# Reordering the weight conversions that run beside the first MLP block, and moving one of them out of the forward transform

## The chip, the core and the metric

The kernel runs on one core of one Trainium2 chip. The metric is the device time of one execution in microseconds (us). Five engines with queues of their own matter here: TensorE (PE, matrix products), VectorE (DVE), ScalarE (ACT), GpSimd (POOL) and SyncE (SP, which only issues transfers).

## The reference, cut to what matters

```python
X = np.fft.rfft(x, axis=1)                      # x: 2 x 3008 x 256
Yr = Xr @ w_r - Xi @ w_i + b_r                  # channel mixing in frequency
Yi = Xr @ w_i + Xi @ w_r + b_i
Yr, Yi = soft_threshold(Yr, 0.01), soft_threshold(Yi, 0.01)
y = np.fft.irfft(Yr + 1j * Yi, n=3008, axis=1)  # 6016 tokens of 256
h = y @ w_in1; y = (h * sigmoid(1.702 * h)) @ w_out1   # 256 -> 2048 -> 256
h = y @ w_in2; y = (h * sigmoid(h)) @ w_out2
```

The four MLP weights are float64 in memory.

## The kernel before

Every product is done in three passes over a rounded part and a remainder (hi x hi, hi x lo, lo x hi). The program has four stages: the forward transform (16 groups g), the mixing (12 units i), the inverse transform (16 steps), and the two MLP layers. PE's order is the order in which the code is written in the MLP; in the transforms a scheduler places the instructions of most engines, except where the code pins an engine's order (POOL and SP in the forward transform, SP in the mixing, PE in the inverse transform). From the second group of the MLP on, all engines follow the written order.

**The MLP.** The tokens are cut into blocks i of 1,024 (the last has 896), and each layer's 2,048 hidden columns into 8 pairs p of 256. A group (layer, block, pair) forms its four hidden quarters from 7 instead of 8 block products: seven products of 3 matmuls (L772), and, for the group before, the second product in 8 pieces of 3 matmuls (L744), so 45 matmuls. Around them: L791 on ACT copies the first product out of PSUM, L793 on DVE adds the second to it (the first hidden quarter). L801 and L803 on ACT copy two more products, and L809 and L812 on DVE add to them. Each quarter then goes through the activation (L775, ACT), is rounded (L777, ACT), and L782 subtracts to get the remainder: on POOL for three quarters, on DVE for one. PE can't go on with the product that reuses a PSUM bank before L803 has emptied it.

**The conversions.** The weights come as 64-bit words, and 32 units (one pair of `w_in` or `w_out` of a layer) are turned into float32 beside the other work, in this order: `w_in` pairs 0 to 3, `w_out` 0 to 4, `w_in` 4 to 7, `w_out` 5 to 7 of layer 1, then layer 2. One unit is a load `raw` from memory (L144 with L145, or L148; SP issues it, there is **one** buffer), L157 on ACT, five bit operations L162 to L166 on DVE, of which L164 and L166 read `raw`, and the final add L219 on POOL. The next unit's load can't start before L166 is done with `raw`. A unit of layer 1 that is kept in SBUF is placed one group later: for `w_in` four small DVE operations L194 to L197 make sums, and L98 (ACT) with L99 (POOL) split it into hi and lo; `w_out` needs L98 and L99 alone. The other units are written back to memory and fetched later.

`CFG['tf']`, `['tm']` and `['ti']` say behind which forward groups, mixing units and inverse steps one unit is converted; `kb` and `kr` do the same for the pairs of the first MLP block and of the later ones (pairs 1 to 6; pairs 1, 3, 5 and 6). The helper `pump(k)` issues k of the five bit operations that wait in the list `fill`, `settle` issues L219, and `hook(h)` is called at six places in a group, with `hook(4)` issuing the next load.

Of the kernel before, what the change touches and what calls it, by code (L numbers as in the profile page):

```python
# [8 lines left out]

F32 = mybir.dt.float32  # L10
CFG = {'lv0': 'V', 'lv': 'VVVVVPVVVVVP', 'dd0': 'VPVVPPPPPVVP', 'dd': 'VVVVVVVVVVPV', 'mpl': 'VPPVVP', 'ths': 'VVVVPV', 'thf': 'PVPVVPVV', 'fsl': 'VPVVVVPV', 'ivf': 'PVVPVVVVVPPVPPVV', 'cva': 'P', 'pol': 'PPPP', 'pil': 'P', 'mvl': 'PVVP', 'xl': 'V', 'xse': 'V', 'gl': 'VPPPPPPP', 'tf': [6, 9, 12], 'tm': [2, 4, 7], 'ti': [2, 5, 9, 13], 'kb': [0, 1, 1, 1, 1, 1, 1, 0], 'kr': [0, 1, 0, 1, 0, 1, 1, 0], 'fa': 3, 'fe': 2, 'xp': [2, 4, 4, 5], 'xq': [1, 4, 1], 'xs': 4, 'xi': [11, 12, 13, 15], 'xsi': 9, 'ca': 4, 'tl': True, 'fwd': 'Pool,SP', 'rest0': 'all', 'rest1': 'all', 'last1': 'all', 'inv': 'PE', 'mid': 'SP', 'last0': 'all', 'thm': 'A', 'gl0': 'PVPVVVPV', 'gl2': 'PPPPPPPP', 'gl3': 'PPPPPPPV', 'xl0': 'V', 'xl1': 'V', 'pre': 17, 'pre2': 0, 'yd': 6, 'nf': 4, 'lvb': 6, 'mlp': 'none', 'pr': 'VVVP', 'pf': 'PV', 'eo': '0000', 'ddb': 6, 'mlp1': 'all', 'mlp2': 'all'}
NUM = dict(tf=[5, 9, 13], tm=[1, 3, 5, 7, 9, 11], ti=[0, 2, 4, 6, 8, 10, 12, 14, 14, 15, 15], kb=[2] * 8, kr=1, fa=3, fe=2, pm=0, nf=4, lvb=6, ddb=8, ivb=1, eob=2, fsb=6, f1=3, f2=0, fm=[7, 8, 9], fi=[1, 1, 2, 2], pre=13, pre2=1, yd=3, psh=0, ie=[12], xp=[1, 3, 4, 5], xq=[1, 2, 2], xs=5, nw=4, xi=[14, 14, 15, 15], xsi=13, rw=2, ca=4, cc=2, tb=1, tmn=1)

DEF = dict(pr="V", pf="V", lv0="V", lv="VPP", dd0="VVVVVP", dd="VPV", mpl="PV", ths="VP", thf="VVPP", fsl="VP", ivf="PPVV", cva="P", pol="P", pil="P", mvl="V", xl="PPVVPPP", xl0="PPVVPPP", xl1="PPVVPPP", xse="VP", gl="P", gl0="P", gl2="P", gl3="P", wcl="V", thc="V", thm="V")
# [7 lines left out]
P = 128  # L22
# [34 lines left out]
def spectral_mlp_kernel(ctx, tc, xin, m0, mfwd, minv, wc, bias, w_in1, w_out1, w_in2, w_out2, outT):  # L57
    nc = tc.nc
# [73 lines left out]
    loaded, bits, added, fill = [], [], [], []  # L132
# [69 lines left out]

    wib_p = []
# [12 lines left out]
    def settle():  # L216
        pump()
        for u, (a, c) in bits:
            E('cva', u[2]).tensor_add(a, a, c)  # L219
            if not u[3]:  # L220
                spilled[u[:3]] = d = dram_p.tile([P, 2 * CU], F32, name=f"w_{u[0]}{u[1]}_{u[2]}")
                nc.sync.dma_start(out=d, in_=a)
        fresh = [(u, a) for u, (a, _) in bits if u[3]]
        done, added[:] = added[:], fresh
        bits[:] = []
        return done

    def window(k, done, now=False):
        for u, a in done:
            if u[0] == "in":  # L230
                for part in place_in(u[1], u[2], a, E('pil', u[2]), sums_tmp):
                    if now:
                        for f in part:
                            f()
                    else:
                        fill.extend(part)
            else:
                place_out(u[1], u[2], a, E('pol', u[2]))
        for _ in range(min(k, len(loaded))):
            u, raw = loaded.pop(0)  # L240
            bits.append((u, cv_bits(raw)))
# [20 lines left out]
    raws, lvs, xs = {}, {}, {}  # L262
# [497 lines left out]
    def group(l, i, p, hook):  # L760
        t0, n = blocks[i]
        func = AF.Silu if l else AF.Gelu_apprx_sigmoid
        w = w_in[l, p]

        y = [[yt[:, mm, t0 + h * n : t0 + (h + 1) * n] for h in range(2)] for mm in range(2)]

        def prod(ps, s, k, first=True):

            xh, xl = xb[l, i, k]
            a, z = w[:, 0, s], w[:, 1, s]  # L770
            for m, (st, mv) in enumerate(((a, xh), (a, xl), (z, xh))):
# [12 lines left out]

        (y1, y3), (y2, y4) = y
        begun = (l, i, p) != (0, 0, 0)
        X, Z, Y = (bank(0, "x")[:, :n] for _ in range(3))
        prod(X, 0, 0)  # L790
        nc.scalar.copy(y1, X)  # L791
        prod(Y, 1, 1)
        nc.vector.tensor_add(y1, y1, Y)  # L793
        hook(1)
        if begun:
            out_next()
        rest(nc.gpsimd, *gate(0, 0, y1))
        hook(2)
        pump(3)
        prod(Z, 3, 2)  # L800
        nc.scalar.copy(y2, Z)  # L801
        prod(X, 4, 3, False)
# [45 lines left out]
    puts = []  # L848
# [12 lines left out]
    for at, (l, i, p) in enumerate(seq):  # L861
        if (l, i, p) in ((0, 0, 1), (0, 0, 2)):
            region(f'mlp{p}')
        if (i, p) == (1, 0):
            region(f'rest{l}')
        if (i, p) == (last, 0):
            region(f'last{l}')
        nxt = (l, i + 1) if i < last else (1, 0)
        more = p == NPR - 1 and (l, i) != (1, last)
        k = rate(at)  # L870

        def hook(h):
            if more:
                if h in (1, 2):
                    for x in ((0,), (1, 2))[h - 1]:
                        xprep(*nxt, x)
                if h == 3:
                    xprep(*nxt, 3, 1)
                if h == 4:
                    xprep(*nxt, 3, 2)  # L880
            if p == 0 and h < 4:
                xprep(l, i, {1: 4, 2: 6, 3: 5}[h])
            if h == 1 and p == NPR - 2 and (l, i) != (1, last):
                xsums(*nxt)
            if h == (3 if len(done) < 2 else 1):
                window(0, done, True)
                done[:] = []
            if h == 1:
                window(k, ())
            if h in (2, 3):  # L890
                moved(h)
            if h == 5:
                fetched[:] = fetch_for(at + 1)
            if h == 4:
                pump()
                cv_load(1 - len(loaded))
            if h == 6:
                done.extend(settle())
                done.extend(added)
                added[:] = []  # L900

        group(l, i, p, hook)
        if (l, i, p) == (0, 0, 0):
            while ydone:
                inv_out()
            closed("iv", "fs")
            wib_p.append(opened("wib", "left", NPR // 2))
        if N('pre2') and (l, i, p) == (0, last, NPR - 1):
            tc.keep_in_program_order(nc.scalar.preload_act_table(AF.Silu))
# [150 lines left out]
```

## Time and profile before

| | us |
|---|---|
| median of three runs (1248.66 to 1253.36) | 1251.43 |
| profiled execution, device time | 1253.26 |
| span of its instructions | 1251.5 |
| PE busy in the span | 1187.8 |
| DVE, ACT, POOL busy | 698.2, 775.6, 587.8 |

The span is divided so: forward transform to about 79, mixing to 158, inverse transform to 220, MLP from 220 to the end. An idle time in brackets in a timeline row is what the engine waited just before that instruction, and for whom.

### The profile page before, as it was taken

How to read it: one execution, taken by the hardware profiler on the slowest of the kernel's cores; microseconds unless marked ns; L12 is line 12 of the kernel's file. 1: busy time of each engine (PE TensorE's matmuls, PEld its weight loads, DVE VectorE, ACT ScalarE, POOL GpSimd, SP SyncE). 2: the span in 40 equal slices, each digit the busy share in tenths (PEclk: the TensorE clock that was granted, in tenths of full speed). 3: DMA queues.
4: the chain of work that ended last, by engine and by line, in shares of the span. 5: the costliest groups of instructions: out<-in, count | busy, mean ns of one | idle time of the engine just before them, and what ended most of it. 6: DMA issues, size and time to landing. Idle time of an engine off the chain costs nothing.

```text
span 1251.5 us, 14934 instructions
## 1 busy us (share of the span) xinstructions
PE 1187.8 (95%) x5220; PEld 969.8 (77%) x5220; DVE 698.2 (56%) x1034; ACT 775.6 (62%) x1481; POOL 587.8 (47%) x465
## 2 busy tenths in 40 slices
PE   7879888777999999999999999999999999999998
PEld 4868678556787887887878987878888888888897
DVE  7899999866735646447446463352352442623522
ACT  3555433656766766767667777666675665765764
POOL 4585553555544444445455774433333333333342
PEclk9989989988999999999999999999999999999999
DMA  8452123011011001001011110000000000000000
GB/s 310 161 183 68 51 71 129 25 46 39 17 49 44 26 34 52 26 26 52 26 59 35 34 43 26 1 32 3 1 35 1 1 34 1 19 16 1 34 1 30
DMA packets 27277, 57.57 MB, mean 46 GB/s; under 512 B 2369, under 2 KB 11585, under 8 KB 25922
## 3 DMA queue, kind: packets, MB, share of 16 engines
q1 hardware_dynamic: 25154, 41.94, 10.2%
q0 software_dynamic: 2048, 14.68, 3.2%
q8 instruction: 41, 0.67, 0.2%
q14 instruction: 34, 0.28, 0.1%
HBM read 44.94 MB, written 11.67 MB: 45 GB/s over the span
## 4 chain that ended last, share of the span: by engine, by line
PE 71%; DVE 15%; ACT 6%; issue 3%; DMA 3%; POOL 1%; SPq 0%; DVEq 0%; ACTq 0%; POOLq 0%
PE o L744 37%; PE x L772 32%; ACT yt L775 1%; DVE f L533 1%; DVE fl L99 1%; PE psf L357 1%; DMA raw<-in_wi 1%; DMA raw<-in_wo 1%; DVE th L519 1%; ACT g L777 1%; DVE cv_c L166 1%; DVE cv_c L165 1%; DVE yt L664 1%; DVE g L782 1%; DVE cv_a L164 1%
## 5 line engine op out<-in xcount | busy, mean ns | idle before, releaser
L782 POOL TENSOR_TENSOR g<-yt,g 128x512 fp32r<-128x512 f32 (+1 forms) x288 | 384.5, 1347 | 538.6 <-DVE g L782 167.5
L744 PE MATMUL o<-g,wo 128*128 128x512 f32 (+1 forms) x2304 | 575.1, 392 | 1.0 <-POOL g L782 0.8
L772 PE MATMUL x<-x,wi 128*128 128x512 f32 (+1 forms) x2016 | 514.0, 394 | 26.5 <-ACT yt L803 22.1
L744 PEld LDWEIGHTS o<-g,wo 128*128 128x128 f32 x2304 | 434.0, 188 | 97.0 <-POOL g L782 1.2
L772 PEld LDWEIGHTS x<-x,wi 128*128 128x128 f32 x2016 | 378.0, 189 | 118.4 <-ACT yt L803 27.8
L775 ACT ACTIVATE yt<-yt 128x512 f32<-128x512 f32 (+1 forms) x288 | 178.9, 621 | 263.4 <-DVE yt L809 216.8
L777 ACT CAST g<-yt 128x512 fp32r<-128x512 f32 (+1 forms) x384 | 234.2, 612 | 11.8
L809 DVE TENSOR_TENSOR yt<-yt,x 128x512 f32<-128x512 f32 (+1 forms) x96 | 64.7, 674 | 264.1 <-PE x L772 264.1
L793 DVE TENSOR_TENSOR yt<-yt,x 128x512 f32<-128x512 f32 (+1 forms) x96 | 64.7, 674 | 143.2 <-ACT yt L791 142.2
L782 DVE TENSOR_TENSOR g<-yt,g 128x512 fp32r<-128x512 f32 (+1 forms) x96 | 68.8, 717 | 69.5 <-ACT g L777 68.5
L695 DVE TENSOR_TENSOR x<-yt,x 128x512 fp32r<-128x512 f32 (+1 forms) x48 | 53.5, 1114 | 24.2 <-ACT x L692 24.2
L812 DVE TENSOR_TENSOR yt<-yt,x 128x512 f32<-128x512 f32 (+1 forms) x96 | 64.8, 675 | 1.9 <-PE x L772 0.5
L775 ACT ACTIVATE yt<-x 128x512 f32<-128x512 f32 (+1 forms) x96 | 56.0, 584 | 3.7 <-PE x L772 3.7
L791 ACT COPY yt<-x 128x512 f32<-128x512 f32 (+1 forms) x96 | 54.8, 571 | 2.6 <-PE x L772 2.5
L803 ACT COPY yt<-x 128x512 f32<-128x512 f32 (+1 forms) x96 | 55.6, 579 | 0.6 <-PE x L772 0.6
L801 ACT COPY yt<-x 128x512 f32<-128x512 f32 (+1 forms) x96 | 54.7, 570 | 0.0
L219 POOL TENSOR_TENSOR cv_a<-cv_a,cv_c 128x512 f32<-128x512 f32 x32 | 47.0, 1469 | 15.9 <-DVE cv_c L166 12.4
L360 PE MATMUL psi<-m,fh 128*128 128x376 f32 (+3 forms) x208 | 49.8, 329 | 2.6 <-DVE sd L514 2.1
L157 ACT ACTIVATE cv_c<-raw 128x512 f32<-128x512 f32 x32 | 21.6, 674 | 43.8 <-DMA raw<-in_wo 23.7
L501 PE MATMUL psm<-wc_hi,xtl 128*128 128x512 f32 x96 | 38.6, 407 | 5.3 <-DVE xtl L99 5.3
L501 PE MATMUL psm<-wc_hi,xth 128*128 128x512 f32 x96 | 39.5, 412 | 3.7 <-ACT xth L98 3.7
L360 PE MATMUL psi<-m,fl 128*128 128x376 f32 (+3 forms) x104 | 34.8, 334 | 6.1 <-DVE fl L99 5.2
(108 smaller groups left out, 1065.7 us busy)
## 6 DMA issues: line engine op xcount, KB each, us to landing
raw<-in_wi SPq DMA_DIRECT2D x32, 256.0 KB, 3.1
raw<-in_wo SPq DMA_DIRECT2D x16, 512.0 KB, 3.6
raw<-in_x SPq DMA_DIRECT2D x12, 512.0 KB, 6.6
out_t<-yt SPq DMA_DIRECT2D x20, 256.0 KB, 2.0
m<-in_mf POOLq DMA_DIRECT2D x4, 1128.0 KB, 7.4
m<-in_mi POOLq DMA_DIRECT2D x4, 1128.0 KB, 7.6
w_out<-cv_a SPq DMA_DIRECT2D x13, 256.0 KB, 2.0
cv_ld<-w_out SPq DMA_DIRECT2D x13, 256.0 KB, 2.6
```

The costliest lines, as they stand in the source:

```text
L360: nc.tensor.matmul(ps, a, z, start=i == 0 and x == 0, stop=i == last and x == 2)
L501: nc.tensor.matmul(t, a, w, start=(n == 0), stop=(n == 11 and grp == 1))
L744: nc.tensor.matmul(acc[h, mm], st, mv, start=first and k == 0, stop=last and k == 2)
L772: nc.tensor.matmul(ps, st, mv, start=first and m == 0, stop=m == 2, skip_group_check=True)
L775: nc.scalar.activation(g, g if src is None else src, func)
L777: nc.scalar.copy(gh, g)
L782: eng.tensor_sub(gl, g, r32(gh))
L791: nc.scalar.copy(y1, X)
L793: nc.vector.tensor_add(y1, y1, Y)
L803: nc.scalar.copy(y3, X)
L809: nc.vector.tensor_add(y2, y2, X)
L812: nc.vector.tensor_add(y3, y3, Z)
```

## The change

It does four things. (1) `tf` loses its last entry and `tm` goes from three entries to four, so that ten units are still converted ahead of the MLP, two instead of three of them behind forward groups. (2) In a group of the MLP all five bit operations are issued in one place ahead of the second half's adds; before, three stood there and two (L165, L166) behind L782 on DVE. (3) While a unit that is kept is being converted (pairs 1 to 6 of the first block), the first quarter's L782 goes to DVE instead of POOL, between the second and third bit operation, and the final add L219 goes to DVE too. (4) Two smaller reorderings: of a placed `w_in` pair the sums' part is split first, and in pair 0 of each block the preparation of the seventh operand moves from hook 2 to hook 3, ahead of the sixth.

```diff
-CFG = {... 'tf': [6, 9, 12], 'tm': [2, 4, 7], ...}
+CFG = {... 'tf': [6, 9], 'tm': [1, 3, 5, 7], ...}
@@ settle
-            E('cva', u[2]).tensor_add(a, a, c)
+            (nc.vector if wib_p and u[3] else E('cva', u[2])).tensor_add(a, a, c)
@@ window
-                for part in place_in(u[1], u[2], a, E('pil', u[2]), sums_tmp):
...
+                sums, puts = place_in(u[1], u[2], a, E('pil', u[2]), sums_tmp)
+                if now:
+                    for f in (*sums, *puts[::-1]):
+                        f()
+                else:
+                    fill.extend(sums + puts)
@@ group
-        rest(nc.gpsimd, *gate(0, 0, y1))
+
+        here = bool(bits) and bits[0][0][3]
+        g11 = gate(0, 0, y1)
+        if here:
+            pump(2)
+        rest(nc.vector if here else nc.gpsimd, *g11)
         hook(2)
-        pump(3)
+        pump()
@@ hook
-            if p == 0 and h < 4:
-                xprep(l, i, {1: 4, 2: 6, 3: 5}[h])
+            if p == 0:
+                for x in {1: (4,), 3: (6, 5)}.get(h, ()):
+                    xprep(l, i, x)
```

In the changed file the lines below the edit carry numbers that are 5 higher: L801, L803, L809 and L812 become L806, L808, L814 and L817.

The first place is the DVE queue in the first MLP block, group of pair 3 (`g` is an activated quarter, `cv_c`, `cv_a` and `raw` belong to the unit being converted, `tmp` to the one being placed). Before, from L793's successor on:

```order
L162 TENSOR_SCALAR cv_c<-cv_c 128x512
L163 TENSOR_SCALAR cv_c<-cv_c 128x512
L164 SCALAR_TENSOR_TENSOR cv_a<-raw_2514,cv_c 128x512
L194 TENSOR_TENSOR tmp<-cv_a 128x128
L195 TENSOR_TENSOR tmp<-cv_a 128x128
L196 TENSOR_TENSOR tmp<-tmp,cv_a 128x128
L197 TENSOR_TENSOR tmp<-cv_a,tmp 128x128
L809 TENSOR_TENSOR yt<-yt,x 128x512
L812 TENSOR_TENSOR yt<-yt,x 128x512
L782 TENSOR_TENSOR g<-yt,g 128x512
L165 TENSOR_SCALAR cv_c<-cv_a 128x512
L166 SCALAR_TENSOR_TENSOR cv_c<-raw_2514,cv_c 128x512
```

In the change the same stretch reads as follows, and goes on with the second half's L782 and L219:

```order
L162 TENSOR_SCALAR cv_c<-cv_c 128x512
L163 TENSOR_SCALAR cv_c<-cv_c 128x512
L782 TENSOR_TENSOR g<-yt,g 128x512
L164 SCALAR_TENSOR_TENSOR cv_a<-raw_2514,cv_c 128x512
L165 TENSOR_SCALAR cv_c<-cv_a 128x512
L166 SCALAR_TENSOR_TENSOR cv_c<-raw_2514,cv_c 128x512
L194 TENSOR_TENSOR tmp<-cv_a 128x128
L195 TENSOR_TENSOR tmp<-cv_a 128x128
L196 TENSOR_TENSOR tmp<-tmp,cv_a 128x128
L197 TENSOR_TENSOR tmp<-cv_a,tmp 128x128
L814 TENSOR_TENSOR yt<-yt,x 128x512
L817 TENSOR_TENSOR yt<-yt,x 128x512
```

L166, which frees `raw`, moved from behind the second half's adds and L782 to ahead of them; the sums L194 to L197 moved behind it, and one L782 came in from POOL.

The second place is the DVE queue in a later block (pair 3 of block 1), where the unit belongs to layer 2. Before:

```order
L163 TENSOR_SCALAR cv_c<-cv_c 128x512
L164 SCALAR_TENSOR_TENSOR cv_a<-raw_3169,cv_c 128x512
L809 TENSOR_TENSOR yt<-yt,x 128x512
L812 TENSOR_TENSOR yt<-yt,x 128x512
L782 TENSOR_TENSOR g<-yt,g 128x512
L165 TENSOR_SCALAR cv_c<-cv_a 128x512
L166 SCALAR_TENSOR_TENSOR cv_c<-raw_3169,cv_c 128x512
```

In the change:

```order
L163 TENSOR_SCALAR cv_c<-cv_c 128x512
L164 SCALAR_TENSOR_TENSOR cv_a<-raw_3169,cv_c 128x512
L165 TENSOR_SCALAR cv_c<-cv_a 128x512
L166 SCALAR_TENSOR_TENSOR cv_c<-raw_3169,cv_c 128x512
L814 TENSOR_TENSOR yt<-yt,x 128x512
L817 TENSOR_TENSOR yt<-yt,x 128x512
L782 TENSOR_TENSOR g<-yt,g 128x512
```

Here only L165 and L166 moved, ahead of the two adds.

The third place is the POOL queue at the end of the forward transform (`wi_...` are placed weight pairs, `xl` is a remainder of the transform's input that PE waits for). Before:

```order
L219 TENSOR_TENSOR cv_a<-cv_a,cv_c 128x512
L99 TENSOR_TENSOR wi_814<-cv_a,wi_814 128x384
L99 TENSOR_TENSOR wi_814<-tmp,wi_814 128x512
L320 TENSOR_TENSOR xl<-dd,xh 128x256
L99 TENSOR_TENSOR wi_1099<-cv_a,wi_1099 128x384
L119 DMA m<-in_mi 128x2268
L219 TENSOR_TENSOR cv_a<-cv_a,cv_c 128x512
L99 TENSOR_TENSOR wi_1099<-tmp,wi_1099 128x512
```

In the change:

```order
L219 TENSOR_TENSOR cv_a<-cv_a,cv_c 128x512
L320 TENSOR_TENSOR xl<-dd,xh 128x256
L99 TENSOR_TENSOR wi_1148<-cv_a,wi_1148 128x384
L119 DMA m<-in_mi 128x2268
L99 TENSOR_TENSOR wi_1148<-tmp,wi_1148 128x512
L219 TENSOR_TENSOR cv_a<-cv_a,cv_c 128x512
L99 TENSOR_TENSOR wi_1267<-cv_a,wi_1267 128x384
```

The two L99 of the first pair left this place (they stand 7 and 4 rows ahead of this L219 now), so L320 follows L219 directly.

## Rows read from the trace of the kernel before

**Rows 1.** The page: span, and busy time of PE with its share.

```profile
span 1251.5 us, 14934 instructions
PE 1187.8 (95%) x5220; PEld 969.8 (77%) x5220; DVE 698.2 (56%) x1034; ACT 775.6 (62%) x1481; POOL 587.8 (47%) x465
```

**Rows 2.** PE's waits over the span: us in total, times, longest.

```profile
PE x L772 <- ACT yt L803: 22.1, 10, 5.1
```

**Rows 3.** Windows: length, busy us (instructions) PE, PEld, DVE, ACT, POOL, clock.

```profile
250.30:266.10 15.80, 12.60 (x45) 9.74 (x45) 10.73 (x13) 8.27 (x16) 9.15 (x7) 0.78 0.16 48
266.10:282.00 15.90, 11.35 (x45) 8.13 (x45) 10.68 (x13) 8.23 (x16) 9.24 (x7) 1.00 0.17 52
282.00:297.80 15.80, 12.19 (x45) 9.43 (x45) 10.76 (x13) 8.19 (x15) 9.25 (x7) 0.89 0.10 35
297.80:309.20 11.40, 8.51 (x30) 6.78 (x31) 6.04 (x10) 7.43 (x13) 6.31 (x5) 0.85 0.13 46
324.00:408.00 84.00, 83.40 (x357) 66.55 (x356) 45.15 (x66) 57.31 (x102) 41.10 (x29) 1.00 0.11 36
```

**Rows 4.** Chain that ended last, 246 to 263: start, us, what.

```profile
246.78 3.44 DMA raw<-in_wi
250.31 0.67 ACT cv_c L157
...
257.88 1.42 DVE g L782
259.29 1.45 DVE cv_c L165
260.77 1.68 DVE cv_c L166
```

**Rows 5.** Timeline of the same group: PE's restart, and ACT.

```profile
253.16 2.93 PE L772 MATMUL x<-x,wi 128*128 128x512 f32 x6 [5.10 <-ACT yt L803]
255.52 0.62 ACT L98 CAST wi<-tmp 128x512 fp32r<-128x512 f32 x1 [2.00 <-DVE tmp L197]
256.56 0.63 ACT L775 ACTIVATE yt<-yt 128x512 f32<-128x512 f32 x1
260.08 0.58 ACT L791 COPY yt<-x 128x512 f32<-128x512 f32 x1
```

**Rows 6.** Lines between 230 and 310: ns minimum/median/maximum of one.

```profile
L165 DVE TENSOR_SCALAR cv_c<-cv_a x5: 421/1516/1516, 243.1 to 304.4; 128x512 uint32<-128x512 uint32 x5
L166 DVE SCALAR_TENSOR_TENSOR cv_c<-raw,cv_c x5: 691/1665/1668, 244.6 to 304.9; 128x512 f32<-128x512 uint32 x5
L194 DVE TENSOR_TENSOR tmp<-cv_a x4: 284/1358/1373, 234.2 to 284.2; 128x128 f32<-128x128 f32 x4
L782 DVE TENSOR_TENSOR g<-yt,g x6: 685/1424/1774, 234.7 to 303.8; 128x512 fp32r<-128x512 f32 x6
L782 POOL TENSOR_TENSOR g<-yt,g x18: 1277/1470/1647, 229.5 to 307.4; 128x512 fp32r<-128x512 f32 x18
L219 POOL TENSOR_TENSOR cv_a<-cv_a,cv_c x5: 1291/1292/1755, 246.4 to 308.6; 128x512 f32<-128x512 f32 x5
L99 POOL TENSOR_TENSOR wi<-cv_a,wi x4: 1010/1049/1058, 239.1 to 285.4; 128x384 fp32r<-128x384 f32 x4
```

**Rows 7.** Timeline of later blocks: block 1 pair 3, block 2 pair 6.

```profile
366.50 0.69 DVE L809 TENSOR_TENSOR yt<-yt,x 128x512 f32<-128x512 f32 x1 [3.14 <-PE x L772]
...
481.18 0.66 ACT L157 ACTIVATE cv_c<-raw 128x512 f32<-128x512 f32 x1 [3.99 <-DMA raw<-in_wi]
...
484.04 1.20 PE L772 MATMUL x<-x,wi 128*128 128x512 f32 x4 [1.98 <-ACT yt L803]
```

**Rows 8.** Timeline at the forward transform's end.

```profile
68.16 5.18 DVE L320 TENSOR_TENSOR xl<-dd,xh 128x256 fp32r<-128x256 f32 x1 [1.38 <-ACT xh L309]
...
72.15 0.44 PE L360 MATMUL psf<-m,xl 128*128 128x376 f32 x1 [1.97 <-POOL xl L320]
```

**Rows 9.** Windows, mixing and inverse transform, columns as in rows 3.

```profile
100.00:220.00 120.00, 106.62 (x535) 93.36 (x534) 117.02 (x178) 51.54 (x96) 60.95 (x53) 0.96 0.24 81
```

More of the change, by code (lines that the diff above doesn't have):

```diff
@@ L10 @@
 F32 = mybir.dt.float32
-CFG = {'lv0': 'V', 'lv': 'VVVVVPVVVVVP', 'dd0': 'VPVVPPPPPVVP', 'dd': 'VVVVVVVVVVPV', 'mpl': 'VPPVVP', 'ths': 'VVVVPV', 'thf': 'PVPVVPVV', 'fsl': 'VPVVVVPV', 'ivf': 'PVVPVVVVVPPVPPVV', 'cva': 'P', 'pol': 'PPPP', 'pil': 'P', 'mvl': 'PVVP', 'xl': 'V', 'xse': 'V', 'gl': 'VPPPPPPP', 'tf': [6, 9, 12], 'tm': [2, 4, 7], 'ti': [2, 5, 9, 13], 'kb': [0, 1, 1, 1, 1, 1, 1, 0], 'kr': [0, 1, 0, 1, 0, 1, 1, 0], 'fa': 3, 'fe': 2, 'xp': [2, 4, 4, 5], 'xq': [1, 4, 1], 'xs': 4, 'xi': [11, 12, 13, 15], 'xsi': 9, 'ca': 4, 'tl': True, 'fwd': 'Pool,SP', 'rest0': 'all', 'rest1': 'all', 'last1': 'all', 'inv': 'PE', 'mid': 'SP', 'last0': 'all', 'thm': 'A', 'gl0': 'PVPVVVPV', 'gl2': 'PPPPPPPP', 'gl3': 'PPPPPPPV', 'xl0': 'V', 'xl1': 'V', 'pre': 17, 'pre2': 0, 'yd': 6, 'nf': 4, 'lvb': 6, 'mlp': 'none', 'pr': 'VVVP', 'pf': 'PV', 'eo': '0000', 'ddb': 6, 'mlp1': 'all', 'mlp2': 'all'}
+CFG = {'lv0': 'V', 'lv': 'VVVVVPVVVVVP', 'dd0': 'VPVVPPPPPVVP', 'dd': 'VVVVVVVVVVPV', 'mpl': 'VPPVVP', 'ths': 'VVVVPV', 'thf': 'PVPVVPVV', 'fsl': 'VPVVVVPV', 'ivf': 'PVVPVVVVVPPVPPVV', 'cva': 'P', 'pol': 'PPPP', 'pil': 'P', 'mvl': 'PVVP', 'xl': 'V', 'xse': 'V', 'gl': 'VPPPPPPP', 'tf': [6, 9], 'tm': [1, 3, 5, 7], 'ti': [2, 5, 9, 13], 'kb': [0, 1, 1, 1, 1, 1, 1, 0], 'kr': [0, 1, 0, 1, 0, 1, 1, 0], 'fa': 3, 'fe': 2, 'xp': [2, 4, 4, 5], 'xq': [1, 4, 1], 'xs': 4, 'xi': [11, 12, 13, 15], 'xsi': 9, 'ca': 4, 'tl': True, 'fwd': 'Pool,SP', 'rest0': 'all', 'rest1': 'all', 'last1': 'all', 'inv': 'PE', 'mid': 'SP', 'last0': 'all', 'thm': 'A', 'gl0': 'PVPVVVPV', 'gl2': 'PPPPPPPP', 'gl3': 'PPPPPPPV', 'xl0': 'V', 'xl1': 'V', 'pre': 17, 'pre2': 0, 'yd': 6, 'nf': 4, 'lvb': 6, 'mlp': 'none', 'pr': 'VVVP', 'pf': 'PV', 'eo': '0000', 'ddb': 6, 'mlp1': 'all', 'mlp2': 'all'}
 NUM = dict(tf=[5, 9, 13], tm=[1, 3, 5, 7, 9, 11], ti=[0, 2, 4, 6, 8, 10, 12, 14, 14, 15, 15], kb=[2] * 8, kr=1, fa=3, fe=2, pm=0, nf=4, lvb=6, ddb=8, ivb=1, eob=2, fsb=6, f1=3, f2=0, fm=[7, 8, 9], fi=[1, 1, 2, 2], pre=13, pre2=1, yd=3, psh=0, ie=[12], xp=[1, 3, 4, 5], xq=[1, 2, 2], xs=5, nw=4, xi=[14, 14, 15, 15], xsi=13, rw=2, ca=4, cc=2, tb=1, tmn=1)
@@ L230, in window @@
             if u[0] == "in":
-                for part in place_in(u[1], u[2], a, E('pil', u[2]), sums_tmp):
[L232 to L236, printed above, removed]
+                sums, puts = place_in(u[1], u[2], a, E('pil', u[2]), sums_tmp)
[4 more added lines that the diff above has]
+                    fill.extend(sums + puts)
             else:
```

## The prediction

> **What bounds the kernel now.** I read the page first. PE is busy for 1187.8 of 1251.5 us [rows 1], so a change can only pay where PE waits or runs at its lower clock. The waits of PE come next: the largest single releaser is L803, the copy that empties a PSUM bank for a first-layer product, with 22.1 us in 10 waits, the longest 5.1 us [rows 2]. Then the windows, cut from one L157 to the next in the first MLP block. Three groups take 15.8 to 15.9 us and a fourth 11.4 us, while a block without trouble has 357 matmuls in 83.40 busy us, 0.2336 us each, or 10.5 us for a group's 45 [rows 3]. So these four groups take 58.9 us where PE needs 42.0: 16.9 us are lost. Another 2.2 us are lost just ahead, since PE's first long wait ended at 253.16 after 5.10 us [rows 5], that is, it began at 248.06, and the windows start at 250.3. The loss is not idle time alone: after that wait six matmuls took 2.93 us where six at full rate take about 1.6, and the granted clock of the three affected windows is 0.78, 0.89 and 0.85 [rows 3, 5].
>
> The chain of the same group says why. The load of `raw` takes 3.44 us to land, and only then can L157 run; DVE then needs the sums, the second half's adds and L782 before it reaches L165 and L166, and L166 ends at 262.4, which is when the next load is issued [rows 4]. Behind L157 stand, on ACT's queue, the gate of the first quarter and the two copies that PE waits for. So the load's round trip (L166 to L157, about 4 us) lies on the path in each group, and what ends last in PE's wait is a transfer that DVE started late.
>
> **The change part by part.**
>
> *The bit operations in one place, first block.* L166 moves ahead of the sums, the adds and L782. In the new order it ends about 5.1 us after L791 starts: L791 0.58 [rows 5], the add 0.7, L775 and L777 0.65 each, L782 0.69, L164 0.69, L165 0.42, L166 0.69 [rows 5 to 7] (L164 is priced as L166, the same operation). With 4 us for the round trip the weights are there after 9.1 us, before the group's 10.5 us are over. The wait for the load therefore leaves the path.
>
> What is late next is ACT. Its casts of the placed weights (L98) stand behind L808 and ahead of the second half's gates, and they need the sums, which now follow L166. The loop from one L791 to the next is: 5.1 to the end of L166, four sums of 0.3 (1.2), three casts at the 0.52 us spacing that the first gate's start shows (1.56), and from that gate's L775 to the next L791 3.52 us (256.56 to 260.08) [rows 5, 6]. Sum 11.4 us. It is the reason why I don't give PE its full 10.5.
>
> *L782 and L219 to DVE.* Rows 6 show that DVE's operations with all operands in SBUF and POOL's exclude each other: L165 takes 0.42 at best and 1.52 as a median, L166 0.69 and 1.67, L194 0.28 and 1.36, DVE's L782 0.69 and 1.42; each waits for about one POOL operation. Taking two of POOL's operations out of the group removes two of these waits (1.0 to 1.1 each) and adds 0.69 twice on DVE. Adding up what both engines need of the shared path in a group that places `w_in`, without any waiting: on DVE L162, L163 and L165 (0.42 each), L164, L166, two L782 and L219 (0.69 each), sums 1.14, together 5.9; on POOL two L782 (1.28 each), L99 of 1.01, 1.29 and 1.29, together 6.2 (the larger L99 priced as L219). That is 12.1 us, above the loop's 11.4, so the period of pairs 2 to 4 lies between 11.4 and, with imperfect packing, 13; I take 12.3.
>
> The Trainium skill, page "Perfetto Trace Analysis", section "Optimizing Scalar/DVE Operations", says of this pair of engines that they share an SBUF port and that moving operations between them might not help. The trace agrees that they exclude each other (1.52 against 0.42 us for L165). By that rule alone the move would be worth nothing: the same addition without it gives 13.2 us, the period would be that, and the total 15.9 us instead of the sum below (1235.5).
>
> *Sum for the first block.* Pair 1's L166 ends about 5.5 us earlier (241 instead of 246.3), but ACT then still has pair 1's three gates behind L157, so PE's wait of 5.1 shortens by only about 2.5. The three groups of 15.8 become 12.3: 10.5. The fourth, which places `w_out` and has no sums, goes from 11.4 to PE's 10.5: 0.9. Together 13.9 us. Bounds: 19.1 if PE is never held (16.9 + 2.2), and 6 in the rival on the port below.
>
> *Later blocks.* L165 and L166 (1.11 clean, 3.2 with a wait each [rows 6]) now stand ahead of the second half's add. Cover: DVE idles 3.14 us there, waiting for PE, in an ordinary group [rows 7], and PE needs that add only 9 matmuls later (2.1 us, less the add's 0.69: 1.4 us more). Cost nothing; without the cover up to 3.2 per group. The gain: with pairs 5 and 6 both converting, pair 6's L157 waits 3.99 us for its load and PE 1.98 for L803 [rows 7]; the load is now issued some 4 us earlier in pair 5. The same wait stands in four blocks; rows 2's 22.1 contain it, and the other three are about 0.6 each, so 3.7 in all. The sixth and seventh operands' order in pair 0 costs nothing, because both are ready before the products that stand last in the group.
>
> *The forward transform's end.* POOL's L320 no longer waits behind two L99; PE waited 1.97 us for it, and DVE's L320 stood 5.18 us instead of 0.41 while POOL ran five operations in a row [rows 8]. So the transform ends about 2 us earlier. But the mixing and inverse transform behind it have DVE busy for 117.02 of 120 us [rows 9], and a fixed amount of DVE work up to the MLP: the two units' sums and bit operations only change places within it, and ACT's cast of the mixing weights still has to wait for a placed pair's add. I take 1.0. Bounds: 4.8 if all of L320's extra time comes back, and a loss of 4 if the moved unit's work (2.6 of bit operations and 1.2 of sums) is not offset by what left the mixing.
>
> *Total.* 13.9 + 3.7 + 1.0 = 18.6 us. The profiled execution took 1253.26, so 1234.7; it lies 1.8 above the median of the runs, 1251.43, and against that the forecast is **1233**.
>
> **The rivals.**
>
> *PE becomes the bound in the first block.* If POOL's and DVE's operations interleave without loss and the casts get their sums in time, all 19.1 come back: 19.1 + 3.7 + 1.0 = 23.8, so 1228. For it speaks that the loop is only 0.9 above PE's 10.5; against it the 12.1 us of port work.
>
> *The port starves DVE.* In the new order POOL has three L99 and two L782 back to back, 6.2 us, just when DVE wants its second L782 and L219. Rows 8 show a DVE operation kept out through five POOL operations (5.18 us); rows 6 show the usual case of one. If each group had the former, L782 would end some 7.5 us after the first cast starts, and L219, the next add and the rest behind it; the period would be 14.7 instead of 12.3, and the block's gain 2.5 + 3.3 + 0.9 = 6.7. With the other terms 11.4: 1240. The Trainium skill, page "SBUF — State Buffer", section "Who interferes with whom", says that whichever of the two starts first keeps the pair for the whole instruction. That gives one wait per POOL operation, as in rows 6; the 5.18 of rows 8 are more than it explains.
>
> *The forward end loses.* With the loss of 4 in place of the gain of 1: 1238.
>
> *Slower than before.* The five bit operations in one place hold up the second half's add in the 16 converting groups of the later blocks. It decides from 4.5 us of extra DVE time (3.14 + 1.4); the change puts 1.1 to 3.2 there. To undo 18.6 us each of the 16 groups would have to lose 1.2 us on PE, so 5.7 us extra on DVE: then about 1252, and 1260 where they lose 1.7. Nothing in the rows shows such a stretch.
>
> **How the numbers follow.** The forecast (1229 to 1237) gets 0.52, PE as the bound 0.18, the starved port 0.20, the loss at the forward end 0.06, slower 0.04. The range takes in PE as the bound with some 3 us more from the forward end (1225) and the starved port with a small loss there (1245). About 0.5% (6 us) is what a measurement here can tell from no change. Faster than 1245.2: the first four cases but for the worst of the starved port, 0.91; within 0.5%: 0.06; slower: 0.03.
>
> **What would show it.** In the first block the waits of L157 for the load vanish, and L157 to L157 goes from 15.8 to about 12.3; PE's waits for the copy (L808 now) shrink from 22.1 to about 6 in all, and some appear on L791 or on `wo`. On DVE L165 and L166 go back to about 0.42 and 0.69, while L782 or L219 become the long ones. In later blocks pair 6's wait of PE is gone. The mixing's first matmul comes 1 to 2 us earlier than 79. Wrong would be: periods near 15 with DVE in long L782, PE waits in the converting groups of later blocks, or an MLP that starts later than 220.

## The result, and the profile after

The changed kernel took 1236.12 us (median of four runs, 1235.41 to 1237.75) against 1251.93 (four runs of the kernel before), a ratio of 0.988 with a 95% interval of 0.986 to 0.990. The forecast was 1233, the range 1225 to 1245. The page of the execution that was profiled (1235.41 us), its first lines:

```profile
span 1233.7 us, 14936 instructions
PE 1182.3 (96%) x5220; PEld 966.4 (78%) x5220; DVE 698.2 (57%) x1046; ACT 776.2 (63%) x1481; POOL 561.8 (46%) x453
```

The span is 17.8 us shorter than in [rows 1]. PE idles 51.4 us of it instead of 63.7, and is busy 5.5 us less for the same matmuls, since its clock was lower in the waiting groups of before. PE's waits in the changed kernel (us in total, times, longest) put a name to the idle part:

```profile
PE psf L357 <- DVE xf L292: 8.5, 3, 5.6
PE psm L501 <- ACT xth L98: 6.0, 1, 6.0
...
PE o L744 <- POOL wo L99: 3.5, 4, 1.9
...
PE x L772 <- ACT yt L808: 2.0, 5, 0.9
PE x L772 <- ACT yt L791: 1.7, 1, 1.7
```

L808 is the copy that was L803; its 22.1 us of [rows 2] are down to 2.0. The windows from L157 to L157 (columns as in [rows 3]) show the same in the first block, from pair 2 to pair 6:

```profile
243.83:258.13 14.30, 12.97 (x48) 10.15 (x49) 10.17 (x16) 10.99 (x20) 8.37 (x7) 0.88 0.21 56
258.13:269.59 11.46, 10.80 (x47) 8.39 (x46) 9.31 (x15) 8.29 (x16) 7.13 (x6) 1.00 0.24 69
269.59:281.03 11.44, 10.75 (x46) 8.36 (x46) 9.31 (x15) 8.26 (x16) 7.10 (x6) 1.00 0.29 70
281.03:291.68 10.65, 10.65 (x48) 8.55 (x47) 8.27 (x11) 7.34 (x14) 5.06 (x5) 1.00 0.14 50
```

The prediction's four windows of 15.80, 15.90, 15.80 and 11.40 us have become 14.30, 11.46, 11.44 and 10.65, the granted clock is back at full in the last three, and in the last PE has no idle time left. L157 now stands elsewhere in its group (in pair 3 it started 6.0 us behind L791 before and starts 0.5 us behind it now), so windows cut at L157 don't hold the same work of PE before and after. To place the gain by stage, the starts of instructions that kept their place are therefore set beside each other: L791, which opens a group, and the last L748, which closes a block.

| stage | before | after | gain | predicted |
|---|---|---|---|---|
| start to the MLP's first L791 | 224.20 | 223.60 | 0.60 | 1.0 |
| to L791 of pair 3 | 35.88 | 34.05 | 1.83 | 2.5 |
| to L791 of pair 6 (pairs 3, 4 and 5) | 47.11 | 33.55 | 13.56 | 10.5 |
| to L791 of pair 7 | 11.42 | 11.38 | 0.04 | 0.9 |
| to the end of the first block | 20.05 | 19.63 | 0.42 | - |
| blocks 1 to 5 | 419.04 | 417.63 | 1.41 | 3.7 |
| blocks 6 to 11 | 489.74 | 490.05 | -0.31 | - |

They add up to 17.55 of the 17.85 us between the two profiled executions. The terms of the first block were priced for windows that are cut at L157, half a group earlier, so they belong to their rows only roughly. Cut at L157, the first block gives 5.87 us ahead of the windows (predicted 2.5), 10.30 in the three (10.5), 0.75 in the fourth (0.9) and a loss of 1.07 behind it; either way it gives 15.85, where the forecast had 13.9. The group of pair 3, rows of DVE, ACT and POOL by start time:

```profile
257.65 0.58 ACT L791 COPY yt<-x 128x512 f32<-128x512 f32 x1
...
259.37 1.41 DVE L163 TENSOR_SCALAR cv_c<-cv_c 128x512 uint32<-128x512 uint32 x1
...
262.01 0.43 DVE L165 TENSOR_SCALAR cv_c<-cv_a 128x512 uint32<-128x512 uint32 x1
262.48 0.69 DVE L166 SCALAR_TENSOR_TENSOR cv_c<-raw,cv_c 128x512 f32<-128x512 uint32 x1
...
264.13 0.62 ACT L98 CAST wi<-tmp 128x512 fp32r<-128x512 f32 x1 [2.88 <-DVE tmp L197]
...
264.83 1.29 POOL L99 TENSOR_TENSOR wi<-tmp,wi 128x512 fp32r<-128x512 f32 x1 [4.33 <-ACT wi L98]
265.60 0.63 ACT L775 ACTIVATE yt<-yt 128x512 f32<-128x512 f32 x1
...
269.11 0.58 ACT L791 COPY yt<-x 128x512 f32<-128x512 f32 x1
```

L157 at 258.13 waits for nothing. The prediction's loop can be read off link by link: L791 to the end of L166 5.5 us (priced 5.1), to the first cast 1.0 (1.2), three casts 1.5 (1.56), from the gate's L775 to the next L791 3.5 (3.52). The sum is exact because these differences cancel; the 0.4 us in the first link come from L163, which took 1.41 us beside POOL's L782 and so held up DVE's. ACT's wait of 2.88 for L197 is the place where the loop closes.

### The profile page after: what moved, and what is told of

Same layout as the page of the kernel before. It is cut to its first block, busy times and chain, and to the rows that moved or that the text cites. A ratio compares the mean times of both kernels' runs of the same rounds, so it can differ in the third digit from the quotient of the medians.

```text
span 1233.7 us, 14936 instructions
## 1 busy us (share of the span) xinstructions
PE 1182.3 (96%) x5220; PEld 966.4 (78%) x5220; DVE 698.2 (57%) x1046; ACT 776.2 (63%) x1481; POOL 561.8 (46%) x453
## 4 chain that ended last, share of the span: by engine, by line
PE 66%; DVE 18%; ACT 8%; issue 5%; DMA 2%; POOL 1%; SPq 0%; DVEq 0%; ACTq 0%; POOLq 0%
PE o L744 35%; PE x L772 31%; ACT yt L775 3%; ACT g L777 2%; DVE f L533 1%; DVE fl L99 1%; DVE cv_a L164 1%; DVE yt L664 1%; DMA raw<-in_wi 1%; DVE th L519 1%; DMA raw<-in_x 1%; DVE cv_c L165 1%; DVE cv_c L162 1%; DVE cv_c L163 1%; DVE yt L793 1%
## 5 line engine op out<-in xcount | busy, mean ns | idle before, releaser
L782 POOL TENSOR_TENSOR g<-yt,g 128x512 fp32r<-128x512 f32 (+1 forms) x282 | 367.9, 1318 | 531.6 <-DVE g L782 260.8
L775 ACT ACTIVATE yt<-yt 128x512 f32<-128x512 f32 (+1 forms) x288 | 179.1, 622 | 279.4 <-DVE yt L814 231.5
L814 DVE TENSOR_TENSOR yt<-yt,x 128x512 f32<-128x512 f32 (+1 forms) x96 | 64.6, 673 | 228.9 <-PE x L772 228.8
L793 DVE TENSOR_TENSOR yt<-yt,x 128x512 f32<-128x512 f32 (+1 forms) x96 | 64.8, 675 | 162.3 <-ACT yt L791 156.3
L782 DVE TENSOR_TENSOR g<-yt,g 128x512 fp32r<-128x512 f32 (+1 forms) x102 | 70.8, 694 | 75.4 <-ACT g L777 75.4
L695 DVE TENSOR_TENSOR x<-yt,x 128x512 fp32r<-128x512 f32 (+1 forms) x48 | 46.9, 976 | 35.8 <-ACT x L692 35.8
L817 DVE TENSOR_TENSOR yt<-yt,x 128x512 f32<-128x512 f32 (+1 forms) x96 | 64.7, 674 | 0.8
L775 ACT ACTIVATE yt<-x 128x512 f32<-128x512 f32 (+1 forms) x96 | 56.2, 586 | 2.2 <-PE x L772 2.2
L808 ACT COPY yt<-x 128x512 f32<-128x512 f32 (+1 forms) x96 | 55.7, 581 | 0.8 <-PE x L772 0.8
L791 ACT COPY yt<-x 128x512 f32<-128x512 f32 (+1 forms) x96 | 54.9, 572 | 2.1 <-PE x L772 2.1
L806 ACT COPY yt<-x 128x512 f32<-128x512 f32 (+1 forms) x96 | 54.9, 572 | 0.0
L219 POOL TENSOR_TENSOR cv_a<-cv_a,cv_c 128x512 f32<-128x512 f32 x26 | 38.0, 1462 | 14.5 <-DVE cv_c L166 10.8
L360 PE MATMUL psf<-m,xh 128*128 128x376 f32 (+1 forms) x160 | 36.3, 323 | 4.3 <-ACT xh L305 3.6
```

The source lines that it names most:

```text
L360: nc.tensor.matmul(ps, a, z, start=i == 0 and x == 0, stop=i == last and x == 2)
```

## The experiments

Ratios are against runs of the kernel before on the same chip, with 95% intervals. The first four experiments ran on one chip, the next four on a second and the last three on a third; the kernel before took 1252.78, 1250.77 and 1248.78 us there (medians), so kernels from different chips are compared by their ratios. In these texts theory A is mine after the result: the gain is the earlier issue of the load.

**The order alone** (kernel before):

```
@@ group
-        pump(3)
+        pump()
```

> The kernel before with one edit alone: all five bit operations of a group stand ahead of the second half's adds. L782 of the first quarter and L219 stay on POOL, and the lists of the conversions stay as before. Theory A (the load of `raw` was the wait, and its earlier issue is the gain): the first block's three periods of 15.8 us fall to 11.8 to 12.2, a little above the changed kernel's 11.45 because one or two DVE operations still wait for POOL; with 1.3 us from the later blocks the time is about 1236 to 1238. Theory B (the port that DVE and POOL exclude each other from is the bound, so that the two operations had to leave POOL): periods of 13.2, 1239 to 1240. Theory C (moving the two operations to DVE is what gained): periods stay above 14.5, 1246 or more.

Measured 1239.12 us (1238.54 to 1239.75), ratio 0.990 (0.987 to 0.992). The periods are 12.48 and 12.49, and the first block, from its first L791 to its end, takes 102.69 us instead of 114.46: 11.8 of the 15.9 that the whole change brings there. Theory A holds by the periods, B and C do not; the period is 0.3 over A's range and the time 1.1 (the time alone would fit B as well). Rows of DVE and POOL show what is left:

```profile
259.69 1.48 POOL L782 TENSOR_TENSOR g<-yt,g 128x512 fp32r<-128x512 f32 x1
260.11 1.61 DVE L164 SCALAR_TENSOR_TENSOR cv_a<-raw,cv_c 128x512 uint32<-128x512 uint32 x1
261.13 1.47 POOL L99 TENSOR_TENSOR wi<-cv_a,wi 128x384 fp32r<-128x384 f32 x1
261.75 1.12 DVE L165 TENSOR_SCALAR cv_c<-cv_a 128x512 uint32<-128x512 uint32 x1
262.91 0.69 DVE L166 SCALAR_TENSOR_TENSOR cv_c<-raw,cv_c 128x512 f32<-128x512 uint32 x1
```

L164 and L165 take 0.9 and 0.7 us more than clean: L164 stands beside POOL's L782, and L165 beside the L99 of a placed pair.

**The two operations on DVE, without the order** (changed kernel, first block):

```
@@ group
-        pump()
+        pump(1 if here else None)
```

> The changed kernel with one edit undone in the first block alone: there L165 and L166 stand again behind the second half's adds and L782; L782 of the first quarter and L219 stay on DVE. Theory A (issue of the load): the load is late again; L166 ends some 2 us earlier than before the change, since fewer DVE operations wait for POOL, so the three periods are 13.3 to 14.3 us and the time is about 1243 to 1246. Theory C (the move of the two operations): periods of 11.5 to 12, 1236 to 1238.

Measured 1248.34 (1247.18 to 1249.86), ratio 0.997 (0.995 to 0.998); periods of 14.43, 14.79 and 14.55. Theory C falls, and A was 0.1 to 0.5 us too hopeful for each period and 2.3 for the time. The rows of DVE and ACT say why:

```profile
259.28 1.51 DVE L165 TENSOR_SCALAR cv_c<-cv_a 128x512 uint32<-128x512 uint32 x1
260.82 1.67 DVE L166 SCALAR_TENSOR_TENSOR cv_c<-raw,cv_c 128x512 f32<-128x512 uint32 x1
...
266.09 0.66 ACT L157 ACTIVATE cv_c<-raw 128x512 f32<-128x512 f32 x1 [4.69 <-DMA raw<-in_wi]
```

In their late place L165 and L166 take as long as in [rows 6]. L165 meets POOL's L99 there (258.76 to 260.50) and L166 the L782 of a later quarter (from 260.46), neither of which was moved. The early place gives them a stretch in which POOL idles (4.33 us ahead of its L99 in the changed kernel).

**The load alone** (kernel before; one unit's load goes into a buffer of its own):

```
+            raw2.append(wib_p[0].tile(...)[:, : 4 * CU].bitcast(mybir.dt.int64))
@@ cv_load
-            raw = cv_p.tile(..., tag="raw", name="raw64", bufs=1)
+            raw = raw2.pop() if raw2 and (kind, l, p) == ("in", 0, 6) else cv_p.tile(...)
```

> The kernel before with the load of one unit (`w_in` pair 6) put into a second buffer, so that neither its load nor the next unit's (pair 7) has to wait for L166; every engine's order is as before, and from the third unit on the one buffer is used again. Theory A (the load is the wait): two of the three periods of 15.8 us fall to 11 to 12.5, the third stays; 1243 to 1245. Theory B (the port is the bound): two periods fall to 13.7 at best, 1247. A rival by which the load is hidden: no period changes, 1251.

Measured 1244.49 (1241.23 to 1247.63), ratio 0.994 (0.992 to 0.996). From L791 to L791 the two groups concerned take 17.20 and 12.54 us instead of 20.94 and 15.78, 3.7 and 3.2 less; the next two stay at 15.69 and 15.64. In ACT's rows the first of these L157 waits for nothing, and the first unit that uses the shared buffer again waits in full:

```profile
255.87 0.67 ACT L157 ACTIVATE cv_c<-raw 128x512 f32<-128x512 f32 x1
...
273.83 0.66 ACT L157 ACTIVATE cv_c<-raw 128x512 f32<-128x512 f32 x1 [5.33 <-DMA raw<-in_wo]
```

One thing in the expectation is not so: in the first of the two groups, which the scheduler still places, L157 came ahead of three of ACT's gates that it had stood behind, and L162 and L163 ahead of L782. The second group, pair 3, has the written order of before on ACT and DVE, and its 3.2 us show the load's round trip as the wait of before.

**The lists of before** (changed kernel, `tf` [6, 9, 12] and `tm` [2, 4, 7] again).

> The changed kernel with the lists `tf` and `tm` of before. Theory A, from the two traces (the MLP starts only 0.2 us earlier in the changed kernel, because the gain at the forward transform's end is lost again in front of the mixing): same time within 1 us, 1236. The prediction's term: 1 us slower, 1237; its bounds 1232 to 1241.

Measured 1235.21 (1234.05 to 1235.43), ratio 0.987 (0.984 to 0.989): 0.9 less than the changed kernel (0.988), with intervals that overlap. (The 0.2 us in the text are by the MLP's first matmul; by its first L791 it is the table's 0.60.) See the forward end below.

**The later blocks split as before** (changed kernel):

```
@@ group
-        pump()
+        pump(None if here else 3)
```

> The changed kernel with the bit operations of the later blocks split as before (three ahead of the second half's adds, two behind L782); the first block stays as changed. By the prediction's term the later blocks lose 3.7 us: 1239 to 1240. By the two traces (blocks 1 to 5 took 409.0 us before and 407.6 after) they lose 1.4: 1237 to 1238, nearly all of it in block 2, where PE's one wait of 1.98 us stood.

(The two sums in this text should read 419.0 and 417.6, as in the table; the difference is right.) Measured 1235.50 (1235.20 to 1237.93), ratio 0.988 (0.987 to 0.990). Blocks 1 to 5 take 417.86 us, 0.2 more than with the new order. Both expectations miss: in this profile the order is worth next to nothing there.

**L782 of the first quarter back on POOL** (changed kernel).

```
@@ group
-        rest(nc.vector if here else nc.gpsimd, *g11)
+        rest(nc.gpsimd, *g11)
```

> The changed kernel with L782 of the first quarter back on POOL; L219 stays on DVE. With both on POOL the first block's period was 12.48, with neither 11.45. If each POOL operation in this place makes one DVE operation wait (about 1.0) and DVE is spared 0.69 by the move, the period is 11.7 to 12.1 and the time 1237 to 1238. If L219 alone made the difference, the period stays at 11.45 and the time within 0.5 of 1236.

Measured 1237.36 (1237.10 to 1237.77), ratio 0.989 (0.988 to 0.991); periods of 11.95 and 11.93. So L782's move is worth 0.5 us of period: L164 takes 1.61 us here and 0.68 in the changed kernel.

```profile
260.78 1.61 DVE L164 SCALAR_TENSOR_TENSOR cv_a<-raw,cv_c 128x512 uint32<-128x512 uint32 x1
262.42 0.43 DVE L165 TENSOR_SCALAR cv_c<-cv_a 128x512 uint32<-128x512 uint32 x1
```

Between b_order's 12.48 and this 11.95 lies another 0.5, but not L219's place alone: the changed kernel also splits the sums' part of a placed pair first, so the L99 that L165 met in b_order (1.12 us) comes later, and L165 takes 0.43. How the 0.5 divides between L219 and this order was not isolated.

**Casts out of the loop** (changed kernel, a version of my own):

```
@@ hook
+            early = len(done) == 1 and k and done[0][0][0] == "in" and done[0][0][3] and bool(wib_p)
...
+                if early:
+                    sums, puts2[:] = place_in(*done[0][0][1:3], done[0][1], E('pil', 0), sums_tmp)
+                    fill[3:3] = sums
+            if h == 3 and early:
+                (kind, l0, p0), a0 = fetched[0]
+                lo = place_out(l0, p0, a0, nc.gpsimd, True)
+                puts2[1]()
+                lo()
+                puts2[0]()
+                done[:] = []
```

Here `place_out` forms the rounded part at once and hands back the subtraction as `lo`; `fill[3:3]` puts the sums behind the third bit operation.

> The changed kernel, in the groups of the first block that place a `w_in` pair: the four sums stand between L164 and L165, the cast of `wo` stands on ACT ahead of the two casts of `wi`, and POOL's subtraction for `wo` ahead of its second one for `wi`. Theory of the loop (sums and three casts stand between L166 and the second half's gate): two casts and 1.1 us of DVE come off the path, the next limit is L814 at 7.05 us behind L791 and then 3.5 to the next L791, so the periods fall from 11.45 to 10.6 to 10.8, and PE's waits for `wo` go; 2.5 to 4 us in all, 1232 to 1234. Rival (the port): POOL's subtractions now start while DVE is at L165 and L166 and keep them out by 1.0 to 1.3 each; periods of 11.4 to 12, 1236 to 1238.

Measured 1231.76 (1230.83 to 1232.76), ratio 0.985 (0.983 to 0.986). Its windows from L157 to L157:

```profile
257.46:267.90 10.44, 10.44 (x47) 8.36 (x46) 9.21 (x15) 8.36 (x16) 7.29 (x6) 1.00 0.21 76
267.90:278.37 10.47, 10.47 (x47) 8.42 (x46) 9.23 (x15) 8.38 (x17) 7.32 (x6) 1.00 0.14 52
```

PE is busy throughout. DVE (x15) and POOL (x6) have as many operations in these windows as in the changed kernel's 11.46. The loop theory is confirmed, down to the next limit: L814 ends 6.9 us behind L791. Periods and time came out a little below the expected ranges.

**The next block's sums later** (the same, and L682, L683 at the end of pair 6):

```
@@ hook
-            if h == 1 and p == NPR - 2 and (l, i) != (1, last):
+            if h == 5 and p == NPR - 2 and (l, i) != (1, last):
```

> As i_first, and the two sums of the next block's operands (L682, L683) are formed at the end of pair 6 instead of ahead of its bit operations. If these 2.6 us of DVE ahead of the five bit operations make what is left of the later blocks' waits (0.31, 0.30, 0.33, 0.60, 1.67 of PE idle in blocks 1 to 5), 1 to 2 us less than i_first: 1231 to 1232. Rival: the sums then stand in front of L793 of pair 7 and PE waits there: 1 to 3 us more than i_first.

Measured 1229.00 (1228.45 to 1230.37), ratio 0.983 (0.981 to 0.985): 2.8 less than i_first, more than expected. Blocks 1 to 5 take 413.74 us, against 417.62 in i_first. In its block 1, pair 6, DVE's rows are

```profile
378.47 0.69 DVE L166 SCALAR_TENSOR_TENSOR cv_c<-raw,cv_c 128x512 f32<-128x512 uint32 x1
379.17 0.69 DVE L814 TENSOR_TENSOR yt<-yt,x 128x512 f32<-128x512 f32 x1
...
381.88 0.68 DVE L682 TENSOR_TENSOR tmp<-yt 128x512 f32<-128x512 f32 x1
382.60 1.73 DVE L683 TENSOR_TENSOR yt<-yt 128x512 f32<-128x512 f32 x1
384.26 0.68 DVE L793 TENSOR_TENSOR yt<-yt,x 128x512 f32<-128x512 f32 x1
```

and in the changed kernel, the same pair with a row of PE from pair 7 behind it:

```profile
376.52 0.96 DVE L682 TENSOR_TENSOR tmp<-yt 128x512 f32<-128x512 f32 x1
377.51 1.67 DVE L683 TENSOR_TENSOR yt<-yt 128x512 f32<-128x512 f32 x1
379.11 1.51 DVE L162 TENSOR_SCALAR cv_c<-cv_c 128x512 f32<-128x512 f32 x1
...
382.92 0.68 DVE L814 TENSOR_TENSOR yt<-yt,x 128x512 f32<-128x512 f32 x1
...
391.84 1.68 PE L772 MATMUL x<-x,wi 128*128 128x512 f32 x6 [0.20 <-ACT yt L808]
```

The two sums come to about 2.6 us ahead of the bit operations and so of L814. Moved behind L782 they stand where DVE idled 2.06 us for L791. The rival shows in the first block alone: there pair 6 gets 1.03 us shorter, but pair 7 takes 6.44 us to the next L791 instead of 5.19, and the block as a whole is 0.8 longer than in i_first.

**The cast in front of the mixing** (changed kernel; the rounded part of one `w_in` pair is formed on POOL):

```
@@ place_in
-        put = lambda k, src: split(w[:, 0, k], w[:, 1, k], src, lo_eng=lo_eng)
+        put = lambda k, src: split(..., hi_eng=nc.gpsimd.tensor_copy if (l, p) == (0, 2) else None, ...)
```

> The changed kernel with the rounded part of one `w_in` pair (the one that is placed in front of the mixing) formed on POOL instead of ACT, so that ACT's cast of the mixing's first operand (xth) no longer stands behind a cast that waits for POOL's L219. If that cast is what gave the forward transform's gain back, PE's wait of 6.0 us in front of the mixing shrinks by 1 to 1.5. What it does to the end: if the mixing and the inverse transform are held by DVE (busy 117.0 of 120 us), the MLP starts no earlier and the time stays within 1 us of 1236; if PE's start counts, 1234.5 to 1235.

Measured 1239.39 (1238.35 to 1242.29), ratio 0.992 (0.990 to 0.994). ACT and PE in the changed kernel, in front of the mixing:

```profile
77.12 0.51 ACT L98 CAST wi<-cv_a 128x384 fp32r<-128x384 f32 x1 [1.20 <-POOL cv_a L219]
77.54 1.13 ACT L98 CAST xth<-xt 128x512 fp32r<-128x512 f32 x2
78.20 1.22 PE L501 MATMUL psm<-wc_hi,xth 128*128 128x512 f32 x2 [6.00 <-ACT xth L98]
```

and in this one:

```profile
75.89 1.24 ACT L98 CAST xth<-xt 128x512 fp32r<-128x512 f32 x2
76.67 1.22 PE L501 MATMUL psm<-wc_hi,xth 128*128 128x512 f32 x2 [4.07 <-ACT xth L98]
79.31 1.22 PE L501 MATMUL psm<-wc_lo,xth 128*128 128x512 f32 x2 [1.41 <-DVE wc_lo L99]
...
195.40 0.89 PE L360 MATMUL psi<-m,fh 128*128 128x376 f32 x2 [3.01 <-DMA m<-in_mi]
```

The cast does hold PE as supposed, and without it the mixing starts 1.5 us earlier. The MLP's first L791 nevertheless comes at 226.27, 2.7 later than in the changed kernel: a wait on DVE stands behind the first matmuls, and in the inverse transform PE waits 3.01 us for a transfer of `m`, which POOL issues and for which the changed kernel doesn't wait. That POOL issues it late because of the casts put on it is likely, but not shown. Neither expectation of the time holds.

**Operands of pair 0 as before** (changed kernel; the seventh operand again at hook 2, the sixth at hook 3).

> The changed kernel with the preparation of the sixth and seventh operand in pair 0 in the order and at the places of before. The prediction prices this reordering at nothing: same time within 0.5 us, 1236. Rival: DVE's and ACT's work for the seventh operand stands again ahead of the copies that PE waits for, and each of the 12 blocks loses 0.2 to 0.4 us: 1238.5 to 1241.

Measured 1235.34 (1234.79 to 1235.68), ratio 0.988 (0.987 to 0.990): by the ratio the same time, blocks 1 to 5 at 417.37 against 417.63. The reordering gains nothing, as priced.

**Everything that helped** (the version with the sums later, with the lists of before).

> i_both with the lists `tf` and `tm` of before. If the parts add, the 0.9 us that a_lists had (1235.21 against 1236.12) come on top of i_both's 1229.0: 1228. If the lists are worth nothing and 0.9 was the spread of runs, 1229.

Measured 1227.18 (1225.93 to 1227.72), ratio 0.982 (0.980 to 0.983). This is the fastest version: some 8 us below the changed kernel by the ratios. What the lists add to it is not clear: the 1.8 us to i_both are between two chips, and the two ratios lie within each other's intervals.

## Why the prediction was right, and where not

**The bit operations in one place** was right in mechanism and chain: the load's wait is gone but for 1.07 us in pair 2, and the loop that was to take its place, 11.4 by the prediction's sum, measures 11.46. b_order, a_split and b_raw2 show that the load's issue was the cause and L166's place the cure.

**L782 and L219 to DVE**: the step that failed is the addition of clean durations, 12.1 us, as a bound for the period above the loop's 11.4, and with it the 12.3. The two groups here that place `w_in`, pairs 3 and 4, take 11.46 and 11.44, and i_first runs the same operations in 10.44. In its rows of DVE and POOL, four such operations in a row:

```profile
274.85 1.31 POOL L99 TENSOR_TENSOR wo<-cv_ld,wo 128x512 fp32r<-128x512 f32 x1
275.68 1.02 DVE L782 TENSOR_TENSOR g<-yt,g 128x512 fp32r<-128x512 f32 x1 [0.75 <-ACT g L777]
276.11 1.47 POOL L99 TENSOR_TENSOR wi<-cv_a,wi 128x384 fp32r<-128x384 f32 x1
276.63 1.50 DVE L219 TENSOR_TENSOR cv_a<-cv_a,cv_c 128x512 f32<-128x512 f32 x1
```

They end 3.28 us after the first began, where the addition has 1.29 + 0.69 + 1.01 + 0.69 = 3.68: in these rows the engines exclude each other for a little less than a row lasts. That the prediction's three windows gave 10.30 against 10.5 all the same is luck: the first, which begins in pair 2, took 14.30, 2.0 more than the 12.3, and the other two 0.85 less each. By whole groups, pairs 3 to 5 gave 13.56; there pair 5 gave most, since it places `w_out`, has no sums and takes 10.65. The first block's 15.85 lie between the forecast's 13.9 and the 19.1 of the rival with PE as the bound, which would have needed the casts out of the loop.

The sentence of the Trainium skill that the prediction weighed ("Perfetto Trace Analysis", section "Optimizing Scalar/DVE Operations": moving operations between these engines might not help) says might, and in this place it did help. Moving L782 alone took 0.5 us off the period (11.95 to 11.46), and b_order, with both operations on POOL, is at 12.48, not at the 13.2 worked out by that rule.

**Pairs 1 and 2**, 2.5, measured 1.83: the wait of 5.10 is gone, but in pair 2 PE now waits 1.95 us for `wo` and 0.58 for L814. **The fourth period**, 0.9, measured 0.75 in its own window, from pair 5 to pair 6. The next, pair 6 by L791, gained 0.04: there L682 and L683 hold up DVE. With these moved (i_both) it is 10.34, which pair 7 loses again.

**Later blocks**, 3.7, measured 1.41, and not for the reason given. Two steps failed. One is the price of nothing for the bit operations ahead of the second half's add. The waits were the load's: L157 of pair 6 waited 2.5 to 4.0 us for it before, and waits for nothing now. But the cover of 3.14 us was read in pair 3. In pair 6 the two sums of 2.6 us use it up, the five operations behind them hold up L814, and pairs 6 and 7 of block 1 take 11.85 and 10.46 us where they took 11.37 and 10.87. i_both, with the sums moved, takes 10.50 and 10.91 there and gains 3.9 us over the blocks 1 to 5.

So the three smaller waits, priced at 1.8 together, gave 0.1, and block 2 gave 1.40 for its 1.98. The other step is taking that one for a wait that the old order always has. Only block 2 had the large wait (1.98; the others 0.54 to 0.63), because L166 met a POOL operation there and took 1.67 us instead of 0.69, so that the load left a microsecond later. In a_later, with the same order but another phase, no such meeting occurred. The three profiles with the old order here have blocks 1 to 5 at 419.05, 418.66 (b_raw2) and 417.86 (a_later), the eight with the new order and the sums unmoved at 417.35 to 417.64: the order is worth 0.2 to 1.7 us, by the phase.

**The forward end**, 1.0, very likely has the wrong sign. In this pair of profiles the MLP's first L791 comes 0.6 earlier. But over all profiles that share the part ahead of it, it comes at 223.25 to 225.45 with the new lists (seven profiles, mean 224.55) and at 221.79 to 224.20 with the old ones (five, mean 223.09), with the same sign on both chips that ran kernels with either. In time the lists make no clear difference: the two pairs of kernels that differ in them alone have ratios of 0.988 and 0.987, and of 0.983 and 0.982, in favour of the old but within each other's intervals. The row that the term rested on is not in every execution: DVE's L320 takes 5.18 us in three of the five profiles with the old lists and in none with the new, but the transform's last matmul ends at 72.6 to 75.3 with the old and at 72.2 to 76.5 with the new.

What is lost stands in front of the mixing. Its first matmul starts at 76.45 to 79.06 with the old lists (mean 77.38) and at 78.00 to 80.23 with the new (mean 79.15); from there to the MLP's first L791 it is 145.1 to 146.8 and 145.2 to 145.6 us. In the changed kernel PE waits 6.00 us there for xth, 3.73 before. a_hi, where this wait is 4.07 and the mixing starts 1.5 earlier, shows that a part of it is ACT's cast behind a placed pair's add. The prediction names such a wait and gives it no price of its own. That the mixing and the inverse transform would swallow an earlier start is not shown, since a_hi also has the 3.01 us for `m`.

So the median's 15.8 us are, by an estimate that sets single profiles beside these means, some 15.9 from the first block, 1.4 from the later ones, and a loss of about 1 to 1.5 ahead of the MLP, where the forecast had 13.9 + 3.7 + 1.0: the surplus of the one made up for part of the other two.

**Signs that were named.** L165 and L166 are back at 0.43 and 0.69 us and L219 is the long one, as foreseen; L782 is not. Lines between 230 and 300, ns minimum/median/maximum:

```profile
L165 DVE TENSOR_SCALAR cv_c<-cv_a x6: 426/427/1406, 238.1 to 297.3; 128x512 uint32<-128x512 uint32 x6
L166 DVE SCALAR_TENSOR_TENSOR cv_c<-raw,cv_c x6: 684/692/694, 239.0 to 297.7; 128x512 f32<-128x512 uint32 x6
L782 DVE TENSOR_TENSOR g<-yt,g x12: 678/693/1440, 233.4 to 294.8; 128x512 fp32r<-128x512 f32 x12
L219 DVE TENSOR_TENSOR cv_a<-cv_a,cv_c x5: 685/1760/1776, 246.2 to 289.6; 128x512 f32<-128x512 f32 x5
```

The waits for `wo` came (3.5 us), the copy's fell further than the 6 forecast.

## What to carry to other kernels

Where one buffer is loaded again and again, place its last reader first, and then write out the loop that takes the wait's place link by link: that sum came out within 0.1 us (its links within 0.4), while an addition of what two engines occupy was no bound. A wait that stands in one block of several can belong to that execution alone, and the idle time that is to cover moved work is to be read in the very group that it moves into. A shift in a stage ahead whose executions scatter by 2 us needs many profiles or a timed pair, not one trace.

## What the runs showed of the hardware

An operation that leaves POOL for DVE, and costs DVE 0.69 us there, still shortened the period by 0.5, since one DVE operation less waits for POOL (L164 at 1.61 us in a_g11 and 0.68 in the changed kernel). DVE's adds that read PSUM (L814, L817) kept their 0.68 to 0.69 us while POOL ran L99 beside them (L814 at 273.65 in i_first, L99 from 273.40 to 274.89).
